# Attention folded into a feed-forward layer on one core: the engines' issue order from a table

## The chip, the core and the metric

One Trainium2 chip, and on it one of its cores. A core has five engines that run side by side, each with an instruction stream of its own: TensorE (PE) for matmuls, VectorE (DVE) and ScalarE (ACT) for elementwise work, GpSimd (POOL), and SyncE (SP), which here only issues DMA transfers. An engine starts its instructions in the order of its stream; where one needs something of another engine it waits, and everything behind it on that engine waits too. The metric is the device time of one execution in microseconds.

## The reference

Eight batches of eight heads of a small attention, whose keys and values are first condensed into 32 memory slots, then a feed-forward layer:

```python
def _attn_ref(q, k, v, phi):                      # 8 x 8 x 576 x 64, phi 8 x 8 x 576 x 32
    a = phi - np.max(phi, axis=2, keepdims=True)  # softmax over the 576 positions
    a = np.exp(a)
    a = a / (np.sum(a, axis=2, keepdims=True) + 1e-09)
    k_m = np.einsum('bhsm,bhsd->bhmd', a, k)
    v_m = np.einsum('bhsm,bhsd->bhmd', a, v)
    scores = scale * np.matmul(q, k_m.transpose(0, 1, 3, 2))
    scores = scores - np.max(scores, axis=-1, keepdims=True)
    attn = np.exp(scores)
    attn = attn / (np.sum(attn, axis=-1, keepdims=True) + 1e-09)
    return np.matmul(attn, v_m)

def _moe_ref(x, w_in, w_out):                     # x 4608 x 512, w_in 512 x 2048, w_out 2048 x 512
    h = x @ w_in
    g = h * np.cos(h)
    return g @ w_out
```

The weights come as 64-bit floats.

## The kernel before

**The algebra.** The output of the attention, attn times v_m, is at once multiplied by w_in. So the kernel multiplies v_m by w_in first (the *fold*, 256 memory slots x 2048 columns for each batch) and the softmaxed scores by the result (the first GEMM, tile `hp`). Then come the cosine (`u`, `gp`) and the second GEMM into three accumulators (`acc`).

**Tiles.** The 4608 tokens are 12 groups of 384 (two batches of 576 are three groups), the 2048 columns 16 pieces `f` of 128. So there are 192 steps (`grp`, `f`). A step is `gemm1` (hp, L519), `act` (L538), `act_end` (L551) and `gemm2` (L564, three accumulators). Names in the text: hp_0_8 is the tile of group 0, piece 8; acc_0_1 the accumulator of group 0's second 128 tokens. Group 0 works in float32, for the weights' scales aren't known yet; all others in pairs of float16 (high and low part), three products for each.

**The cosine.** ACT rounds hp to whole periods (`gp` as integers, L544); DVE takes the difference (`u`, L547); ACT takes the sine (L552); DVE multiplies by hp (L554 in group 0, L556 later), which frees hp's PSUM buffer (three in all, `ps_h`). From group 1 on ACT copies the high half (L558) and DVE subtracts for the low half (L559); then gp can be multiplied. The sine and the exponential of the softmaxes need different function tables on ACT, so a change between them costs a table load.

**The weights.** w_in and w_out come in eight pieces each, through three raw buffers in turn (two pieces of w_in use room in `wo` instead). `to_float32` (L134) turns a piece into float32: DVE takes the sign (L143), ACT the low bits (L147), ACT scales the high word (L151), DVE joins both (L152), ACT squares for the largest value (L154), into the raw buffer, which is free for the next load after that. When all of w_in is squared, `weight_scale` (L174) finds one scale (L177 to L182, L164 to L171: `m_in`, `e_in`, `s_in`), and `scales` (L323) the factor `T` from it. The float16 pairs are made by `split_first` (L499: vw_0_q from vf_q), `fold` (L481: vw_b_q from pv), `w_in_split` and `w_out_split`.

**The first batch's fold.** `fold_first(j)` (L487) multiplies the condensed values of batch 0 by piece j of w_in into a PSUM tile (`pvf`) and copies it into `vf` (L497), two pieces to a `vf` tile. The copies of pieces 0 and 1 are on ACT by name; for the other six `nc.any` lets the scheduler take an engine. In the profile ACT has four of the eight and DVE four. Group 0's three output copies (L589) are `nc.any` as well; the profile has two on ACT and one on DVE.

**Attention.** `memory(b)` (L227) and `attend(b)` (L349) are generators that the main loop (L709) advances between the steps: the softmax over positions (L254, L260), the condensing matmuls (psA), their transpose (tpx, km, vm), the scores (sc), their softmax (L389 to L400) and the transposition back (aT). All these small PSUM tiles, and pvf and pv, share two buffers (`ps_s`).

**The order.** The code is written as one program. A scheduler of the framework puts each engine's instructions in order when the program is built: it models the engines, and takes among the instructions whose inputs are there the one of highest priority, mostly the earliest in the program. A few are pinned by `tc.keep_in_program_order`: the warm-up matmuls (L630), two conversion steps of piece 1, the subtraction L254 from batch 4 on, and the rounding L544 behind the last step of a group.

**Startup.** The first 14 `warm` matmuls, and more between the small ones of batch 0, multiply zeros: their results aren't used, they keep PE busy while it would wait.

Of the kernel before, what the change touches and what calls it, by code (L numbers as in the profile page):

```python
# [16 lines left out]
AF = mybir.ActivationFunctionType  # L17
ALU = mybir.AluOpType
# [13 lines left out]
WS = 256  # L32
# [7 lines left out]
EXP_MASK = 0x7F800000  # L40
NT = 4
LAG = 4


@with_exitstack
def attention_then_ffn(ctx: ExitStack, tc: tile.TileContext, phi, phiT, kv, qT, w_in, w_out, eye, out):
    nc = tc.nc
# [32 lines left out]
    loads, st = {}, {}  # L80
# [53 lines left out]
    def to_float32(dst, raw, sq_to, pin=False, after_sign=None):  # L134

        low, high = raw[:, :, :, 0], raw[:, :, :, 1]
        flat = raw.rearrange("p c f t -> p c (f t)")
        halves = dst.bitcast(I16).rearrange("p c (f t) -> p c f t", t=2)  # L140
        low_top = flat.bitcast(U8).rearrange("p c (f t) -> p c f t", t=8)[:, :, :, 3]
        high_top = flat.bitcast(I8).rearrange("p c (f t) -> p c f t", t=8)[:, :, :, 7]
        sign = nc.vector.tensor_scalar(out=halves[:, :, :, 1], in0=high_top, scalar1=0.0, scalar2=-32768.0,  # L143
                                       op0=ALU.is_lt, op1=ALU.mult)
        if after_sign:
            after_sign(sign)
        begin = nc.scalar.activation(halves[:, :, :, 0], low_top, AF.Copy, scale=2.0 ** -5, bias=-31.0 / 64.0)  # L147
        if pin:
            for ins in (sign, begin):
                tc.keep_in_program_order(ins)  # L150
        nc.scalar.activation(high.bitcast(F32), high.bitcast(F32), AF.Copy, scale=2.0 ** -112)  # L151
        nc.vector.scalar_tensor_tensor(out=dst.bitcast(I32), in0=high, scalar=3, in1=dst.bitcast(I32),  # L152
                                       op0=ALU.logical_shift_left, op1=ALU.bitwise_or)
        nc.scalar.activation(low.bitcast(F32), dst, AF.Square, accum_out=sq_to)  # L154
# [72 lines left out]
    def memory(b):  # L227
        a = loads.pop(("phi", b))
# [10 lines left out]
        if b < NT:  # L239
# [3 lines left out]
            top = small_ps(f"top_{b}")[:, 0:HM]  # L243
            for g in range(2):
                nc.tensor.matmul(top[:, g * P:(g + 1) * P], lhsT=nmx[:, g:g + 1].broadcast_to([P, P]), rhs=ident,
                                 start=True, stop=True)
        else:
            top = st["top", b]
# [2 lines left out]
            yield  # L251
            yield
        for c0, c1, n in ((0, 2, P), (2, 4, P), (4, 5, S - 512)) if b == 0 else ((0, 4, P), (4, 5, S - 512)):
            ins = nc.vector.tensor_tensor(out=a[:n, c0:c1], in0=a[:n, c0:c1],  # L254
                                          in1=top[:n].unsqueeze(1).broadcast_to([n, c1 - c0, HM]),
                                          op=ALU.subtract)
            if b >= NT:

                tc.keep_in_program_order(ins)
            nc.scalar.activation(a[:n, c0:c1], a[:n, c0:c1], AF.Exp)  # L260
        yield
        if b:
# [3 lines left out]
        for c, (s0, n) in enumerate(TCH):  # L266
            for g in range(2):
                for j in range(4):
# [3 lines left out]
                        lhsT=a[:n, c, h * M:(h + 1) * M], rhs=kvs[c][:n, h * KV:(h + 1) * KV],  # L272
                        start=(c == 0 and g == 0), stop=(c == 4), skip_group_check=True)
# [7 lines left out]
        pv = psA[:, 0:2 * KV].rearrange("p (g x) -> p g x", g=2)  # L281
# [205 lines left out]
    def fold_first(j):  # L487
        q, r = divmod(j, 2)
        if r == 0:
            st["vf", q] = wk.tile([P, 2, FS], F32, tag="vw", name=f"vf_{q}", bufs=8)  # L490
        pv = small_ps(f"pvf_{j}").rearrange("p (g x) -> p g x", g=2)
        for g in range(2):
            for i in range(2):
                c = 2 * g + i
                nc.tensor.matmul(pv[D * i:D * (i + 1), g], lhsT=st["vm", 0][:, c],
                                 rhs=w_in_sb[:, c, j * WS:(j + 1) * WS], start=True, stop=True)
        (nc.scalar.copy if j < 2 else nc.any.tensor_copy)(out=st["vf", q][:, :, r * WS:(r + 1) * WS], in_=pv)  # L497

    def split_first(q):  # L499
        vw = wk.tile([P, 2, 2, FS], F16, tag="vw", name=f"vw_0_{q}", bufs=8)  # L500
# [37 lines left out]
    def act(grp, f, hp, pin=False):  # L538
        u = ew.tile([P, GT], F32, tag="u", name=f"u_{grp}_{f}", bufs=3)
        gp = ew.tile([P, GT], F32, tag="gp", name=f"gp_{grp}_{f}", bufs=6)  # L540
        ni = gp.bitcast(I32)
        for b, t0, c0, n in regions(grp):
            c, cu = slice(c0, c0 + n), st["cu", b] if grp else 1.0 / (2.0 * math.pi)
            ins = nc.scalar.activation(ni[:, c], hp[:, c], AF.Copy, scale=cu, bias=0.25)  # L544
            if pin:
                tc.keep_in_program_order(ins)
            nc.vector.scalar_tensor_tensor(out=u[:, c], in0=hp[:, c], scalar=cu, in1=ni[:, c],  # L547
                                           op0=ALU.mult, op1=ALU.subtract)
        return u, gp
# [12 lines left out]
    accs = {}  # L562
# [21 lines left out]
    def evacuate(grp, t):  # L584
# [1 line left out]
        ob = wk.tile([P, DM], F32, tag="back", name=f"ob_{grp}_{t}", bufs=4)  # L586
        osc = st["os_mid", pair] if 3 * r + t == 4 else st["os", 2 * pair + (3 * r + t) // 5] if grp else None
        if grp == 0:
            nc.any.tensor_copy(out=ob, in_=accs[grp][t])  # L589
        elif grp == 11 and t == 2:  # L590

            r0, m = (3 * grp + t) * P, DM // 2
# [34 lines left out]

    def warm(n):
        for _ in range(n):
            tc.keep_in_program_order(nc.tensor.matmul(wps, lhsT=zeros[:, 0:P], rhs=zeros, start=True, stop=True))  # L630
    warm(14)
    mem = memory(0)
    next(mem)
# [8 lines left out]
    warm(3)  # L642

    def attention_rest(sign):
        tc.keep_in_program_order(sign)
        next(mem)
        warm(2)

# [147 lines left out]
```

## Time and profile before

| | us |
|---|---|
| median of three runs | 708.84 |
| lowest, highest | 708.61, 710.9 |
| the profiled execution, whole | 710.08 |
| its span, first to last instruction | 708.3 |
| PE busy in it | 687.8 (97%) |
| DVE busy | 532.7 (75%) |
| ACT busy | 518.7 (73%) |

The profile is one execution. Its span leaves out what lies ahead of the first and behind the last instruction, 1.8 us here. A row of a time line gives the start, the length, the engine, the line of the code, the operation, the tiles (out<-in) and the count of instructions merged into it; in brackets stands how long the engine had been idle and who ended that. A float32 matmul is two records of PE, so `x8` of hp in group 0 is four matmuls, two tiles. The ends of matmuls are modelled; their starts are measured.

### The profile page before, as it was taken

What the parts mean: (1) busy time and instruction counts of PE and PEld (TensorE: products, weight loads), DVE (VectorE), ACT (ScalarE), POOL (GpSimd) and SP (SyncE); (2) the same over time, 40 slices, a digit from 0 to 9 for tenths busy, and PEclk for the clock granted to TensorE, in tenths of its full rate; (3) what the DMA queues carried; (4) which work ended last, traced back from release to release, by engine and by line L of the source; (5) the groups of instructions that cost most, each with busy time, mean ns of one, the idle gap of its engine ahead of it and who ended that gap; (6) DMA issues with size and microseconds to landing.
All of it is one profiled execution on the core that took longest, in us unless ns stands there. A gap on an engine that the chain in (4) does not pass through costs nothing.

```text
span 708.3 us, 11822 instructions
## 1 busy us (share of the span) xinstructions
PE 687.8 (97%) x4597; PEld 364.7 (51%) x4597; DVE 532.7 (75%) x1135; ACT 518.7 (73%) x951; POOL 13.7 (2%) x34
## 2 busy tenths in 40 slices
PE   8699899999999999999999999999999999999997
PEld 3354345565555445666445445666445454665553
DVE  3889879999968966599667886599567976575552
ACT  1899999897985865778666875778766875665652
POOL 0000000000000000000000100000000000000000
PEclk9999999999999999999999999999999999999999
DMA  8996782326407100160105200160100000100101
GB/s 281 379 321 218 266 293 60 105 61 195 146 1 237 44 1 1 56 226 1 44 1 167 99 16 1 46 206 31 44 2 2 22 23 1 46 1 1 45 1 44
DMA packets 31959, 66.18 MB, mean 93 GB/s; under 512 B 2208, under 2 KB 12320, under 8 KB 31904
## 3 DMA queue, kind: packets, MB, share of 16 engines
q1 hardware_dynamic: 27440, 57.43, 25.0%
q10 hardware_dynamic: 4464, 8.00, 3.0%
q8 instruction: 36, 0.59, 0.3%
q14 instruction: 19, 0.16, 0.1%
HBM read 51.79 MB, written 9.44 MB: 86 GB/s over the span
## 4 chain that ended last, share of the span: by engine, by line
PE 60%; DVE 21%; ACT 16%; DMA 2%; issue 1%; ACTq 0%; POOL 0%; DVEq 0%; SPq 0%
PE acc L577 33%; PE hp L533 16%; DVE u L547 4%; ACT u L552 3%; DVE u L556 3%; DVE gp L559 3%; PE psA L270 3%; DVE vw L478 2%; PE sc L376 2%; PE pv L471 2%; ACT gp L558 2%; DMA phi<-in_phi 2%; DVE wo L191 2%; PE hp L524 1%; DVE w_in_parts L202 1%
## 5 line engine op out<-in xcount | busy, mean ns | idle before, releaser
L577 PE MATMUL acc<-wo,gp 128*128 128x512 f16 x1584 | 371.8, 379 | 1.2 <-DVE ob L589 0.7
L577 PEld LDWEIGHTS <-gp 128*128 128x128 f16 x1584 | 153.3, 98 | 162.6 <-issue 4.1
L533 PE MATMUL hp<-aT,vw 128*128 128x192 f16 (+1 forms) x1440 | 202.7, 284 | 1.0 <-DVE u L556 1.0
L533 PEld LDWEIGHTS <-vw 128*128 128x128 f16 x1440 | 128.3, 98 | 77.4 <-issue 17.5
L552 ACT ACTIVATE u<-u,quarter 128x384 f32<-128x384 f32 x192 | 116.7, 615 | 63.8 <-DVE u L547 62.9
L556 DVE SCALAR_TENSOR_TENSOR u<-hp,u 128x384 f32<-128x384 f32 x176 | 96.5, 553 | 60.6 <-ACT u L552 60.1
L544 ACT ACTIVATE gp<-hp,cu 128x192 int32<-128x192 f32 (+1 forms) x240 | 115.4, 492 | 28.1 <-PE hp L533 12.3
L547 DVE SCALAR_TENSOR_TENSOR u<-hp,cu,gp 128x192 f32<-128x192 f32 (+1 forms) x240 | 118.8, 503 | 21.9 <-ACT gp L544 21.5
L559 DVE TENSOR_TENSOR gp<-u,gp 128x384 f16<-128x384 f32 x176 | 96.4, 552 | 43.0 <-ACT gp L558 41.9
L558 ACT CAST gp<-u 128x384 f16<-128x384 f32 x176 | 88.8, 510 | 54.3 <-DVE u L556 53.0
L572 PE MATMUL acc<-wo,gp 128*128 128x512 f32 x96 | 45.1, 599 | 0.0
L478 DVE SCALAR_TENSOR_TENSOR vw<-pv,vw 128x512 f16<-128x512 f32 x48 | 31.5, 684 | 3.0 <-ACT vw L477 2.9
L524 PE MATMUL hp<-aT,vf 128*128 128x384 f32 x64 | 25.6, 533 | 7.9 <-DVE vf L497 3.1
L477 ACT ACTIVATE vw<-pv 128x512 f16<-128x512 f32 x48 | 26.8, 589 | 1.1 <-PE pv L471 0.9
L572 PEld LDWEIGHTS acc<-wo,gp 128*128 128x128 f32 x96 | 17.4, 190 | 17.8 <-issue 15.2
L601 ACT ACTIVATE ob<-acc,os 128x512 f32<-128x512 f32 x27 | 17.8, 682 | 9.6 <-PE acc L577 7.1
L524 PEld LDWEIGHTS hp<-aT,vf 128*128 128x128 f32 x64 | 12.2, 202 | 20.1 <-issue 4.3
L552 ACT ACT_TABLE_LOAD x17 | 21.8, 1283 | 0.3
L270 PE MATMUL psA<-kv,phi 128*32 128x129 f32 (+1 forms) x640 | 21.0, 275 | 0.7 <-ACT phi L260 0.5
L376 PE MATMUL sc<-q,km 128*64 128x256 f32 (+3 forms) x192 | 19.8, 342 | 1.6 <-DVE vw L478 1.2
L270 PEld LDWEIGHTS psA<-kv,phi 128*32 128x32 f32 (+1 forms) x640 | 16.4, 109 | 7.3 <-issue 3.3
L376 PEld LDWEIGHTS sc<-q,km 128*64 128x64 f32 x192 | 12.1, 140 | 12.0 <-issue 3.6
(136 smaller groups left out, 544.7 us busy)
## 6 DMA issues: line engine op xcount, KB each, us to landing
kv<-in_kv SPq DMA_DIRECT2D x32, 516.0 KB, 6.9
raw_out<-in_w_out SPq DMA_DIRECT2D x8, 1024.0 KB, 5.8
q<-in_qT SPq DMA_DIRECT2D x7, 1152.0 KB, 6.0
out<-ob ACTq DMA_DIRECT2D x30, 256.0 KB, 2.1
raw_in<-in_w_in SPq DMA_DIRECT2D x6, 1024.0 KB, 8.1
phi<-in_phi SPq DMA_DIRECT2D x8, 512.0 KB, 5.9
w_in_sb<-w_in_parts SPq DMA_DIRECT2D x12, 256.0 KB, 4.0
kv<-in_kv SPq DMA_DIRECT2D x8, 258.0 KB, 8.5
```

Of the source, the lines that this page charges most:

```text
L270: nc.tensor.matmul(psA[32 * j:32 * (j + 1), g * KV:(g + 1) * KV], lhsT=a[:n, c, h * M:(h + 1) * M], rhs=kvs[c][:n, h * KV:(h + 1) * KV], s ...
L376: nc.tensor.matmul(sc[D * p:D * (p + 1), g * n:(g + 1) * n], lhsT=km[:, 2 * g + p], rhs=qt[:, 2 * g + p, t0:t0 + n], start=True, stop=True)
L478: nc.vector.scalar_tensor_tensor(out=vw[:, 1, g], in0=src, scalar=T, in1=vw[:, 0, g], op0=ALU.mult, op1=ALU.subtract)
L533: nc.tensor.matmul(hp[:, c0:c0 + n], lhsT=vw[:, wi, g, fo * P:(fo + 1) * P], rhs=aT[:, ai, g, c1:c1 + n], start=(k == 0), stop=(k == 5))
L544: ins = nc.scalar.activation(ni[:, c], hp[:, c], AF.Copy, scale=cu, bias=0.25)
L547: nc.vector.scalar_tensor_tensor(out=u[:, c], in0=hp[:, c], scalar=cu, in1=ni[:, c], op0=ALU.mult, op1=ALU.subtract)
L552: nc.scalar.activation(u, u, AF.Sin, scale=TWO_PI_BELOW, bias=quarter)
L556: nc.vector.scalar_tensor_tensor(out=u, in0=hp[:, :GT], scalar=2.0 ** -17, in1=u, op0=ALU.mult, op1=ALU.mult)
L558: nc.scalar.copy(gp[:, 0], u)
L559: nc.vector.tensor_tensor(out=gp[:, 1], in0=u, in1=gp[:, 0], op=ALU.subtract)
L572: nc.tensor.matmul(accs[grp][t], lhsT=gp[:, t * P:(t + 1) * P], rhs=wo[:, f + 1], start=(f == 0), stop=(f == NF - 1))
L577: nc.tensor.matmul(accs[grp][t], lhsT=gp[:, gi, t * P:(t + 1) * P], rhs=parts[:, wi], start=(f == 0 and gi == 0 and wi == 0), stop=(f == N ...
```

## The change

A table `NEXT` holds, for each of the five engines, a string of numbers. `issue_in_order`, called at the end of the program, takes an engine's instructions in program order as a list, and for each number removes the instruction at that place of what is left; each is tied to the one before it, without a semaphore. So the table fixes the whole order on every engine: 4029 matmuls, 931 instructions of ACT, 1136 of DVE, 30 of POOL and 107 of SP. `5x3` stands for three fives; `0` is the next one in program order. The pins go, and the two free choices of an engine are written out: six fold copies on DVE (ACT keeps two), group 0's output copies on ACT.

```diff
+NEXT = {
+    mybir.EngineType.PE: (
+        "0x26 8 0x8 8 0x16 2x8 4x8 0x4 3x2 5x4 0x3 2x4 0x24 4x2 12x2 0x4 14x2 54x2 0x8 58 0x2 56 0x4 63 52 "
...
+    mybir.EngineType.Activation: (
+        "0 1 0x5 3 2 1x2 3x2 6 0x2 1 11 3 1 9 1 0 3 0 5 2 4 8x2 4x2 2 0 1x2 7 4 1 0 2 7 3 2 0x2 3 0 7 0 4 3 0 "
...
+    mybir.EngineType.DVE: (
+        "6x2 5 0x2 1x2 0x12 4 1x2 0 1 4x3 0 3 11 3x2 10 3 8 0 2 6 2 3 2 5 2 17 19 2 3 17 0x3 10 14 10 20 0x2 "
...
+    mybir.EngineType.SP: (
+        "0x29 6x4 0x2 4x2 0 3 0x5 16 0 1 0x14 2x2 0x6 2x2 0x6 2x2 0x6 2x2 0x6 2x2 0x12 "),
+}
+
+def issue_in_order(tc):
+    traced = [i for i in tc.nc.cur_bb.bb.instructions if not type(i).__name__.startswith("BassTile")]
+    for engine, text in NEXT.items():
+        left = [i for i in traced if i.engine == engine]
+        last = None
+        for word in text.split():
+            at, _, times = word.partition("x")
+            for _ in range(int(times or 1)):
+                ins = left.pop(int(at))
+                if last is not None:
+                    tc.add_manual_dep(ins, last.name, mybir.DependencyInfo(
+                        mybir.DependencyClass.NoSync, mybir.DependencyReason.DATA), reason="issue order")
+                last = ins
+        assert not left, engine
...
-        begin = nc.scalar.activation(halves[:, :, :, 0], low_top, AF.Copy, scale=2.0 ** -5, bias=-31.0 / 64.0)
-        if pin:
-            for ins in (sign, begin):
-                tc.keep_in_program_order(ins)
+        nc.scalar.activation(halves[:, :, :, 0], low_top, AF.Copy, scale=2.0 ** -5, bias=-31.0 / 64.0)
...
-        (nc.scalar.copy if j < 2 else nc.any.tensor_copy)(out=st["vf", q][:, :, r * WS:(r + 1) * WS], in_=pv)
+        (nc.scalar.copy if j < 2 else nc.vector.tensor_copy)(out=st["vf", q][:, :, r * WS:(r + 1) * WS], in_=pv)
...
-            nc.any.tensor_copy(out=ob, in_=accs[grp][t])
+            nc.scalar.copy(out=ob, in_=accs[grp][t])
...
-            tc.keep_in_program_order(nc.tensor.matmul(wps, lhsT=zeros[:, 0:P], rhs=zeros, start=True, stop=True))
+            nc.tensor.matmul(wps, lhsT=zeros[:, 0:P], rhs=zeros, start=True, stop=True)
...
     for p in pending:
         gemm2(*p)
+    issue_in_order(tc)
```

Crossed off against the program order, parts of the table read so (line, tile; in0 is piece 0 of w_in, out0 of w_out):

```
DVE, from batch 0's values on: L301, L302 vm_0; L143 in0; L308; L381 sc_0_0, sc_0_256; L389; L152 in0;
  L390; L143 in1; L394; L395; L143 out0; L396; L152 in1; L310; L400; L152 out0; L406 x3; L143 in2;
  L406; L242 nmx_1; L143 in3; L547 u_0_0; L152 in2, in3; ev_0; L554 gp_0_0; L547 u_0_1, u_0_2;
  L554 gp_0_1; L547 u_0_3; L497 pvf_2; ...
ACT, from km_0 on: L147 in0; L151 in0; L147 in1; L422; L497 pvf_0; L151 in1; L147 out0; L151 out0; L147 in2;
  L154 in0, in1, out0; L147 in3; L151 in2; L544 gp_0_0; L151 in3; L552 u_0_0; L497 pvf_1; L544 gp_0_1;
  L154 in2, in3; L552 u_0_1; L544 gp_0_2, gp_0_3; L552 u_0_3, u_0_2; L147 out1; ...
PE: ... 14 warm; pvf_0; 6 warm; hp_0_0, hp_0_1; pvf_1; hp_0_2, hp_0_3; pvf_2; sc_0_384; acc; top_1; acc; pvf_3;
  acc x2; hp_0_4; psA_1; hp_0_5; acc; tpx_1; acc x3; sc_1_0; hp_0_6; acc; sc_1_256; acc; sc_1_512; acc; pvf_4;
  acc x2; hp_0_7; half of hp_0_8; acc x2; pvf_5; acc; hp_0_9; the other half of hp_0_8; acc x5; hp_0_10; ...
```

In groups 1 to 11 the table mixes the three accumulators of several pieces: the nine matmuls of a piece, which the program has together, stand in packs of three with other pieces between.

More of the change, by code (lines that the diff above doesn't have):

```diff
@@ L42 @@
 LAG = 4
+NEXT = {
+    mybir.EngineType.PE: (
[31 rows of a table added]
+    mybir.EngineType.Activation: (
[18 rows of a table added]
+    mybir.EngineType.DVE: (
[23 rows of a table added]
+    mybir.EngineType.Pool: (
+        "0x2 2 0x3 2 0 1 0 2 0x2 3 0 1 0 3 0x3 3 0x3 3 0x4 "),
+    mybir.EngineType.SP: (
[15 more added lines that the diff above has]
+        assert not left, engine
 @with_exitstack
@@ L253, in memory @@
         for c0, c1, n in ((0, 2, P), (2, 4, P), (4, 5, S - 512)) if b == 0 else ((0, 4, P), (4, 5, S - 512)):
[L254 to L259, printed above, removed]
+            nc.vector.tensor_tensor(out=a[:n, c0:c1], in0=a[:n, c0:c1],
+                                    in1=top[:n].unsqueeze(1).broadcast_to([n, c1 - c0, HM]),
+                                    op=ALU.subtract)
             nc.scalar.activation(a[:n, c0:c1], a[:n, c0:c1], AF.Exp)
@@ L543, in act @@
             c, cu = slice(c0, c0 + n), st["cu", b] if grp else 1.0 / (2.0 * math.pi)
-            ins = nc.scalar.activation(ni[:, c], hp[:, c], AF.Copy, scale=cu, bias=0.25)
-            if pin:
-                tc.keep_in_program_order(ins)
+            nc.scalar.activation(ni[:, c], hp[:, c], AF.Copy, scale=cu, bias=0.25)
             nc.vector.scalar_tensor_tensor(out=u[:, c], in0=hp[:, c], scalar=cu, in1=ni[:, c],
@@ L644, in attention_rest @@
     def attention_rest(sign):
-        tc.keep_in_program_order(sign)
         next(mem)
```

69 rows, old and new, of the table NEXT are left out of this document.

## The prediction

> **What bounds the kernel now.** I read the page first, then the waits of PE, busy time by stages, and last the time lines of PE, DVE and ACT over the first 125 us.
>
> ```profile
> span 708.3 us, 11822 instructions
> ...
> PE 687.8 (97%) x4597; PEld 364.7 (51%) x4597; DVE 532.7 (75%) x1135; ACT 518.7 (73%) x951; POOL 13.7 (2%) x34
> ```
>
> No matmul is added or dropped, so PE's 687.8 us stay. An order can win at most the other 20.5 us, and what a slow clock stretches. The stages say where these are (per row: stage, length, busy us of PE, PEld, DVE, ACT, POOL, granted clock, DMA share, GB/s):
>
> ```profile
> 20.00:40.00 20.00, 13.03 (x55) 6.12 (x55) 15.98 (x24) 18.49 (x24) 0.00 (x0) 0.95 1.05 367
> ...
> 120.00:160.00 40.00, 39.27 (x261) 22.95 (x260) 39.88 (x82) 37.50 (x77) 0.31 (x1) 1.00 0.30 73
> 160.00:700.00 540.00, 536.72 (x3773) 288.25 (x3772) 397.07 (x856) 379.58 (x725) 10.05 (x19) 1.00 0.17 56
> 700.00:708.30 8.30, 4.42 (x21) 1.80 (x19) 1.24 (x2) 1.16 (x2) 0.00 (x0) 0.93 0.26 95
> ```
>
> Idle PE: 7.0 us from 20 to 40, 0.7 from 120 to 160, 3.3 from 160 to 700 and 3.9 at the tail; the rest, 5.6, lies before 20 and at one wait near 75. From 20 to 40 ACT is 18.5 of 20 us busy, from 120 to 160 DVE 39.9 of 40: PE waits there for engines that have no room. After 160 us PE is full and the other two have a quarter free. The waits of PE that an order can touch (who, for whom; us in total, times, longest):
>
> ```profile
> PE hp L524 <- DVE vf L497: 3.1, 1, 3.1
> ...
> PE hp L524 <- DVE gp L554: 2.1, 1, 2.1
> ...
> PE hp L524 <- ACT vf L497: 1.8, 1, 1.8
> PE sc L376 <- DVE vw L478: 1.2, 1, 1.2
> PE hp L533 <- DVE u L556: 1.0, 2, 0.8
> ...
> PE acc L577 <- DVE ob L589: 0.7, 1, 0.7
> ...
> PE acc L577 <- ACT ob L601: 0.4, 1, 0.4
> ```
>
> The first three lie in the first 80 us, the other four (3.3 us) behind 120; with smaller ones the stages have 4.0 there.
>
> **The change, part by part.** I crossed the table off against the program order and walked the three full engines through it by hand, each instruction starting at the later of its engine's last end and its inputs, with the durations of these rows (ns of one; back to back on one engine the next starts some 100 ns before the end):
>
> ```profile
> L552 ACT ACT_TABLE_LOAD x17 | 21.8, 1283 | 0.3
> ...
> L147 ACT ACTIVATE wo<-raw_out 128x1024 int16<-128x1024 uint8 x8 | 10.9, 1368 | 0.0
> ...
> L152 DVE SCALAR_TENSOR_TENSOR wo<-raw_out,wo 128x1024 int32<-128x1024 int32 x8 | 9.8, 1227 | 1.4 <-ACT raw_out L151 1.2
> L154 ACT ACTIVATE raw_out<-wo 128x1024 f32<-128x1024 f32 x8 | 9.3, 1161 | 0.0
> L151 ACT ACTIVATE raw_out<-raw_out 128x1024 f32<-128x1024 f32 x8 | 9.2, 1147 | 0.0
> ...
> L143 DVE TENSOR_SCALAR wo<-raw_out 128x1024 int16<-128x1024 int8 x8 | 6.0, 751 | 0.0
> ...
> L497 DVE COPY vf<-pvf 128x512 f32<-128x512 f32 x4 | 2.7, 677 | 0.0
> ...
> L497 ACT COPY vf<-pvf 128x512 f32<-128x512 f32 x4 | 2.3, 574 | 0.0
> ```
>
> **Fold copies and group 0's output copies.** Of the eight fold copies ACT has four now and two afterwards: DVE gains 2 x 0.68 = 1.35 us, ACT loses 2 x 0.57 = 1.15. One of three ob copies goes back from DVE to ACT, 0.57 to 0.68. Net DVE +0.7, ACT -0.6, where both are full. Exp and Sin alternate 34 times in the new ACT order, as many as the table loads now: no price. SP's queue keeps its order but for a few kv pieces of batch 2 moved behind weight pieces; no load of the first 47 us can move, since they land one behind the other.
>
> **From the first weight piece to the first GEMM.** These rows of before carry it:
>
> ```profile
> 18.71 1.37 ACT L147 ACTIVATE w_in_sb<-raw_in 128x1024 int16<-128x1024 uint8 x1 [1.12 <-DMA raw_in<-in_w_in]
> ...
> 22.22 1.22 DVE L152 SCALAR_TENSOR_TENSOR w_in_sb<-raw_in,w_in_sb 128x1024 int32<-128x1024 int32 x1
> ...
> 26.99 2.82 PE L524 MATMUL hp<-aT,vf 128*128 128x384 f32 x8 [0.92 <-DVE aT L406]
> ...
> 35.50 0.61 ACT L552 ACTIVATE u<-u,quarter 128x384 f32<-128x384 f32 x1
> ...
> 38.44 1.98 PE L495 MATMUL pvf<-w_in_sb,vm 128*64 128x256 f32 x8
> ...
> 50.66 1.56 PE L524 MATMUL hp<-aT,vf 128*128 128x384 f32 x4
> ```
>
> In the table DVE does the sign of piece 0 (L143) ahead of the score transposes: 18.7 to 19.4; transposes to 20.5, maximum to 21.4, then L152 of piece 0 to 22.7, 0.8 us sooner, and with it the first fold. But the subtraction of the softmax comes behind, then L152 of pieces 1 and of w_out's 0 come ahead of the normalization's end, and a sign step between the last transposes: aT is ready at 31.8, not 27.0. The first GEMM starts 4.8 us later. ACT doesn't lose that: it converts meanwhile, takes up hp_0_0 at 35.1, loads Sin and ends the first sine at 38.4 (now 36.1), with 2.9 us more of conversion done than it has now at that point. PE's lag at fixed points: pvf_2 at 41.5 against 38.4, hp_0_5 at 52.4 against 50.7.
>
> [...]
>
> **The stall at 72 us** is the clearest waste of the scheduler's order:
>
> ```profile
> 71.25 1.13 PE L572 MATMUL acc<-wo,gp 128*128 128x512 f32 x2
> ...
> 74.80 0.67 DVE L497 COPY vf<-pvf 128x512 f32<-128x512 f32 x1
> ...
> 75.52 4.54 PE L524 MATMUL hp<-aT,vf 128*128 128x384 f32 x8 [3.14 <-DVE vf L497]
> ```
>
> The copy of pvf_4, whose matmuls ended at 68.3, stands on DVE behind eight other things. In the table it follows L152 of piece 5 at once, 69.3 by my walk, and PE has hp_0_7 and accumulations until then: 3.1 us of idleness and 4.54 - 2.82 = 1.7 of slow clock go. At 78.7 PE has what it has now at 79.9, where the two hp are through: the lag of 1.7 has become a lead of 1.2.
>
> **To the first split-precision GEMM.** What is late next is a chain on ACT. Piece 7 of w_in loads into the buffer that the square (L154) of w_out's piece 3 frees; that ended at 79.0, now 82.6, since ACT first waits 1.7 us for a transpose of batch 1 and 1.0 for the sign of w_out's piece 3. hp_0_10 waits 0.7 us for gp_0_7, which frees its PSUM buffer, and gp_0_9 costs 1.0. Between the steps of the w_in scale (L179 to L182) the table has L152 and L143 of w_out's pieces 5 and 6, so s_in comes at 101.2, not 97.2; the last split of vw_0_0 at 111.9, not 107.1.
>
> ```profile
> 79.04 0.37 SPq L124 DMA_DIRECT2D raw_in<-in_w_in  x1
> ...
> 79.90 5.31 PE L572 MATMUL acc<-wo,gp 128*128 128x512 f32 x12
> ...
> 97.05 0.15 DVE L171 TENSOR_SCALAR s_in<-s_in 128x1 f32<-128x1 f32 x1
> ...
> 105.67 1.40 DVE L478 SCALAR_TENSOR_TENSOR vw<-vf,T,vw 128x512 f16<-128x512 f32 x2
> ...
> 107.87 1.15 PE L533 MATMUL hp<-aT,vw 128*128 128x192 f16 x12
> ```
>
> So hp_1_0 starts at 112.0 against 107.9 (4.1 later), with 38 accumulations of group 0 behind it instead of 36; two of them are 4 of the 12 records that start in 5.2 us from 79.90, 1.7 us. **Net +2.4 us.** The walk has some 250 steps; an error of 2 us in either direction would not surprise me.
>
> **From 112 us on** I only measured distances in the table, in PE's own time. A quiet step shows what a tile needs:
>
> ```profile
> 691.63 1.14 PE L533 MATMUL hp<-aT,vw 128*128 128x384 f16 x6
> ...
> 694.97 0.56 DVE L556 SCALAR_TENSOR_TENSOR u<-hp,u 128x384 f32<-128x384 f32 x1 [0.68 <-ACT u L552]
> ...
> 696.11 0.56 DVE L559 TENSOR_TENSOR gp<-u,gp 128x384 f16<-128x384 f32 x1 [0.58 <-ACT gp L558]
> ```
>
> From the end of hp (692.8) to the free buffer 2.8 us, to gp 3.9. In the table the shortest ways are 3.9 and 4.5, most are above 6. Accumulators have 2.6 us or more to be copied out, psA_2 stands 6.5 us behind its maximum. So of the 4.0 us of late idleness I let 3.0 go. New tight places are sc_2_0 and sc_5_0, one accumulation (0.65) behind their tpx, and folds split in two: +0.8, between 0 and 2. The last matmul to the end stays: 3.9.
>
> **Sum**: +2.4 - 3.0 + 0.8 = +0.2 on the profiled span of 708.3. The profiled execution took 710.08 with what lies around it, the median of the runs is 708.84. **Forecast: 709.0 us.**
>
> **The rivals.** *Faster (702)*: my walk is too slow where ACT waits for DVE. Of its ACT idleness from 42 to 76 us (5.8 against 1.7 now) most hangs on single inversions, as u_0_3 ahead of u_0_2 (1.1) and the wait for back_1_0 (1.7). If the real durations let these fall together, the lead of 1.2 at 79 us grows to 4 and holds to hp_1_0; with -3 behind 110 that is -7. For it: PE's waits of 3.1, 2.1 and 1.8 are all inversions of the scheduler, and ACT is given 0.6 less. Against it: ACT and DVE, not PE, are full from 20 to 160 us.
>
> *Slower (714)*: DVE's lag is not absorbed. It is 39.88 of 40 us busy from 120 to 160 and gets 0.7 more. If it enters this stretch 4.8 us late, as at vw_0_0 in my walk, it can't catch up before 160 us. Now gp_1_0 is ready at 117.3 and used at 125.2, 7.9 us of room:
>
> ```profile
> 116.79 0.55 DVE L559 TENSOR_TENSOR gp<-u,gp 128x384 f16<-128x384 f32 x1
> ...
> 125.21 0.81 PE L577 MATMUL acc<-wo,gp 128*128 128x512 f16 x3
> ```
>
> The table uses gp_1_0 some three steps behind its hp; from a lag of about 6 us on PE waits for each gp, and all of the lag counts: +6 behind hp_1_0 instead of +2.4, and with half of the late waits left +5.
>
> *The table changes nothing*: if it were the scheduler's own order written out, 708.8. Its PE order differs by eye in the first ten rows (psA's chunks 1 to 4 without fillers between), so this has no chance of its own and lies within the forecast's.
>
> **How the numbers follow.** The measurement can't tell changes under 0.3% (2.1 us) apart. Within (706.7 to 711.0), my forecast: 0.38. Faster: 0.36; the walk's error of 2 us and the late waits reach it easily. Slower: 0.26. The range takes in 702 at the lower side and 714 at the upper: 702 to 714; the likeliest case alone spans 706.7 to 711.
>
> **What would show it.** The walk is right if the first hp of L524 starts near 32 us with 5 us or more of idleness ahead, if no PE wait for vf stands near 72 us, and if the first L533 comes near 112 us; wrong if that one comes ahead of 107. The late part is right if PE's waits behind 120 us sum to about 1.6 us. The slow rival shows as L577 waiting for gp between 115 and 165 us.

## The result and the profile after

The changed kernel took 713.91 us (median of five runs, 712.71 to 716.14), the kernel before 710.9 beside it (five runs, 708.61 to 712.01): 1.0056 times as long, 95% interval 1.0031 to 1.0081. In a second series, 712.98 against 709.6: 1.0044, interval 1.0029 to 1.006. So it is slower by 3 to 4 us, where 709.0 us and practically no difference (+0.2 us) were forecast.

The lines of the new helper push every line behind it down: the copies of fold tiles are now L591, the first GEMM L618 and L627, accumulations L664 and L669, the conversion L243 to L251. First the page of the changed kernel:

```profile
span 712.4 us, 11883 instructions
...
PE 689.3 (97%) x4597; PEld 362.9 (51%) x4597; DVE 530.6 (74%) x1136; ACT 517.2 (73%) x950; POOL 14.5 (2%) x34
```

PE has the same work; this execution's span is 4.1 us longer than the one shown of the kernel before. The same stages as before (length, then busy us of PE, PEld, DVE, ACT, POOL, the granted clock, DMA share, GB/s):

```profile
20.00:40.00 20.00, 13.50 (x63) 5.99 (x63) 16.56 (x28) 17.63 (x22) 0.99 (x1) 0.91 1.06 372
120.00:160.00 40.00, 39.70 (x257) 23.13 (x256) 39.77 (x81) 38.82 (x80) 0.31 (x1) 1.00 0.42 100
160.00:700.00 540.00, 536.91 (x3777) 287.41 (x3776) 396.07 (x860) 379.75 (x730) 10.32 (x19) 1.00 0.17 56
```

Behind 160 us PE is idle for 540 - 536.91 = 3.1 us, where it was 3.3. The forecast had let 3.0 us of late idleness go. The waits of PE say what took its place (who, for whom; us in total, times, longest):

```profile
PE hp L618 <- DVE aT L500: 4.7, 1, 4.7
PE psA L364 <- DMA kv<-in_kv: 3.2, 3, 1.8
PE hp L618 <- ACT vf L591: 3.0, 1, 3.0
...
PE acc L664 <- DVE gp L646: 1.4, 2, 1.0
...
PE hp L627 <- DVE u L648: 1.3, 2, 1.0
PE pv L565 <- DVE vl L437: 1.0, 1, 1.0
PE pv L565 <- DVE vm L396: 0.6, 1, 0.6
```

Of the four late rows of before, that of `sc` behind `vw` and the two of `ob` are gone. The last three rows here (2.9 us) are new or, that of `u`, at new places. Of the start, PE's time line:

```profile
33.19 4.52 PE L618 MATMUL hp<-aT,vf 128*128 128x384 f32 x8 [4.69 <-DVE aT L500]
37.63 1.08 PE L589 MATMUL pvf<-w_in_sb,vm 128*64 128x256 f32 x8
41.74 2.85 PE L618 MATMUL hp<-aT,vf 128*128 128x384 f32 x8 [3.02 <-ACT vf L591]
...
69.14 1.08 PE L589 MATMUL pvf<-w_in_sb,vm 128*64 128x256 f32 x8
70.15 1.98 PE L664 MATMUL acc<-wo,gp 128*128 128x512 f32 x4
71.97 2.10 PE L618 MATMUL hp<-aT,vf 128*128 128x384 f32 x6
...
110.75 2.84 PE L664 MATMUL acc<-wo,gp 128*128 128x512 f32 x6 [0.98 <-DVE gp L646]
113.43 1.15 PE L627 MATMUL hp<-aT,vw 128*128 128x192 f16 x12
```

The first GEMM comes 6.2 us later than before (26.99), the stall at 72 us is gone, and hp_1_0 starts at 113.43 instead of 107.87. Two accumulations more lie behind it by then (1.7 us), so this one execution has lost 5.56 - 1.7 = 3.8 us at hp_1_0, and from there to the end only 0.3 more of its 4.1.

### The profile page after: what moved, and what is told of

The parts are those of the page before. It is cut to its first block, busy times and chain, and to the rows that moved or that the text cites. A ratio compares the mean times of both kernels' runs of the same rounds, so it can differ in the third digit from the quotient of the medians.

```text
span 712.4 us, 11883 instructions
## 1 busy us (share of the span) xinstructions
PE 689.3 (97%) x4597; PEld 362.9 (51%) x4597; DVE 530.6 (74%) x1136; ACT 517.2 (73%) x950; POOL 14.5 (2%) x34
## 4 chain that ended last, share of the span: by engine, by line
PE 75%; ACT 12%; DVE 10%; DMA 2%; issue 1%; SPq 0%; ACTq 0%
PE acc L669 45%; PE hp L627 22%; PE pv L565 3%; PE psA L364 2%; PE sc L470 2%; DMA kv<-in_kv 2%; ACT u L644 2%; DVE u L639 1%; ACT raw_out L251 1%; DVE vw L572 1%; ACT raw_in L251 1%; DVE u L648 1%; ACT gp L638 1%; ACT raw_out L248 1%; ACT L644 1%
## 5 line engine op out<-in xcount | busy, mean ns | idle before, releaser
L669 PE MATMUL acc<-wo,gp 128*128 128x512 f16 x1584 | 372.0, 379 | 0.0
L669 PEld LDWEIGHTS <-gp 128*128 128x128 f16 x1584 | 151.4, 98 | 168.4 <-issue 10.2
L627 PE MATMUL hp<-aT,vw 128*128 128x192 f16 (+1 forms) x1440 | 198.2, 283 | 1.3 <-DVE u L648 1.3
L627 PEld LDWEIGHTS <-vw 128*128 128x128 f16 x1440 | 129.8, 98 | 72.9 <-issue 9.9
L638 ACT ACTIVATE gp<-hp,cu 128x192 int32<-128x192 f32 (+1 forms) x240 | 114.1, 491 | 51.2 <-PE hp L627 31.7
L644 ACT ACTIVATE u<-u,quarter 128x384 f32<-128x384 f32 x192 | 115.7, 612 | 41.4 <-DVE u L639 40.4
L664 PE MATMUL acc<-wo,gp 128*128 128x512 f32 x96 | 46.2, 604 | 1.4 <-DVE gp L646 1.4
L618 PE MATMUL hp<-aT,vf 128*128 128x384 f32 x64 | 25.2, 527 | 7.9 <-DVE aT L500 4.7
L664 PEld LDWEIGHTS acc<-wo,gp 128*128 128x128 f32 x96 | 17.0, 190 | 19.9 <-issue 14.4
L618 PEld LDWEIGHTS hp<-aT,vf 128*128 128x128 f32 x64 | 12.1, 200 | 20.5 <-ACT w_in_sb L247 5.2
L693 ACT ACTIVATE ob<-acc,os 128x512 f32<-128x512 f32 x27 | 17.9, 684 | 4.2 <-PE acc L669 3.9
```

Of the source, the lines that this page charges most:

```text
L627: nc.tensor.matmul(hp[:, c0:c0 + n], lhsT=vw[:, wi, g, fo * P:(fo + 1) * P], rhs=aT[:, ai, g, c1:c1 + n], start=(k == 0), stop=(k == 5))
L644: nc.scalar.activation(u, u, AF.Sin, scale=TWO_PI_BELOW, bias=quarter)
L664: nc.tensor.matmul(accs[grp][t], lhsT=gp[:, t * P:(t + 1) * P], rhs=wo[:, f + 1], start=(f == 0), stop=(f == NF - 1))
L669: nc.tensor.matmul(accs[grp][t], lhsT=gp[:, gi, t * P:(t + 1) * P], rhs=parts[:, wi], start=(f == 0 and gi == 0 and wi == 0), stop=(f == N ...
```

## The experiments

Each kernel below differs from the kernel before or from the changed one only in what is said; the order of all instructions not named is written out as it stood there. "Before" always means runs of the kernel before on the same chip in the same series. In a list of moves, `A > B` means that A now stands ahead of B in its engine's queue.

### Which part of the change costs?

**The old order, written as a table.** Nothing else is changed.

```diff
-    (order by the scheduler)
+NEXT = {...}            # the scheduler's order, engine by engine
+    issue_in_order(tc)
```

> The kernel before with its own order, instruction by instruction on every engine, written as a table, and its own engine for every copy. Every theory: no difference that can be measured (ratio 0.997 to 1.003), since only the way in which the order is written differs. The profile is a second sample of the loads: if the later landing of the first kv pieces under the change (the last at 16.0 us, 14.2 before) is chance from run to run, a value anywhere between may come here; if the change causes it, it stays at 14.2 +- 0.4.

Measured: ratio 0.9994 (interval 0.9982 to 1.0006). The form of the table costs nothing. The last kv piece landed at 14.93 us.

**The copies alone.**

```diff
-        (nc.scalar.copy if j in (0, 1, 2, 6) else nc.vector.tensor_copy)(out=st["vf", q]...   # what before came to
+        (nc.scalar.copy if j < 2 else nc.vector.tensor_copy)(out=st["vf", q]...
-            (nc.vector.tensor_copy if t == 1 else nc.scalar.copy)(out=ob, ...
+            nc.scalar.copy(out=ob, ...
```

> The order before, with only the copies changed: pvf_2's and pvf_6's copies on VectorE, ob_0_1's on ScalarE, each at the place in the new engine's queue that the old order gives it. By the prediction (VectorE +0.7 us, ScalarE -0.6, where both are full): 0 to +0.7 us. Rival: ahead of the stall at 72 us VectorE's queue is the critical one, so that a copy of 0.68 us more in it costs its whole length, +0.7 to +1.4 us.

Measured: 0.9983 (0.9973 to 0.9993), 1.2 us *faster*. Both expectations missed; which copy did it is tested further on.

**Both halves of the order.** One kernel takes the table up to hp_1_0 and the old order behind it, the other the reverse; the sets of instructions ahead of that point differ by a dozen. Each half brings its own engines for the copies: the fold copies go with the start, the output copies with the rest.

> The table's order up to the first split-precision GEMM (hp_1_0), the order before for all that is left. Theory start: the changed kernel loses its 3.8 us ahead of hp_1_0 and its rest is worth nothing, so this one is as slow as the changed kernel, +3 to +5 us against before. Theory rest (the table's rest costs what the start doesn't): +0 to +2 us. Landings: the last kv piece near 16.0 us if the new start causes it.

> The order before up to hp_1_0, the table's for all that is left. Theory start: within 1 us of before. My prediction had the rest at -2.2 us: then 706.5 to 707 where before is at 709. Theory rest: +2 to +4 us. PE's waits behind 120 us sum to 3 us as in the changed kernel (theory start), or to 1.6 (prediction).

Measured: new start 1.0061 (1.0044 to 1.0077), +4.3 us; new rest 1.0016 (1.0003 to 1.0028), +1.1 us. The start carries the loss, and the rest is no gain either. The halves do not simply add up: the first has two new waits at 127 and 129 us, 2.5 us in all, where group 0's output copies, ordered as before, follow a late start. With the last kv piece at 14.78 us, the late landing in the changed kernel's first profile (16.0) isn't something that the new start always brings.

**The changed kernel again.**

> The changed kernel unchanged, for a second profile and more runs. Start and rest measured by halves gave +4.3 and +1.1 us; if they add up, +5.4 us against before; if part of the start's loss is made good later, +3 to +4. The last kv piece landed at 16.0 us in the profile of the changed kernel, at 14.2 to 14.9 in the five others. Chance: it lands at 14 to 15 us here and the first GEMM starts near 31.5; cause: at 16 again and 33.

Measured: 1.0044 as told above, the last kv piece at 14.56, the first GEMM at 31.26 and hp_1_0 at 111.51: here the start has lost 111.51 - 107.87 - 1.7 = 1.9 us, and the span (710.4) is 2.1 longer than before's. So between 1.9 and 3.8 us go at the start in these two executions, and 0.2 to 0.3 behind it. The 1.9 between them goes with the landing of the first loads (the last kv piece at 14.56 and 16.0 us), which differs between these two executions of the same kernel.

### The start: what is the late first GEMM worth?

**The chain to aT put back**, in the changed kernel:

```
VectorE:  L484 at > L249 in0;   L488, L489, L490, L494, L500 x4 > L243 in1, L243 out0, L249 in1, L249 out0
ScalarE:  L516 at (exp) > L247 in1
```

> The changed kernel with one chain put back as it stood before: on VectorE the softmax of the first head block (subtraction, sum, reciprocal, product, four transposes) ahead of the conversions of pieces 1 and of w_out's piece 0, on ScalarE its exp ahead of the conversion of piece 1. First GEMM near 27 us instead of 31 to 33. Theory idle start: PE's 4 us of lateness count whole, -3 to -4 us against the changed kernel. Rival, as my prediction had it: ScalarE and VectorE are full from 20 to 100 us, and ScalarE takes up hp_0_0 no sooner for it, so 0 to -1 us; the lateness shows at the next waits of PE instead.

Measured: 1.0104 (1.0087 to 1.012), 716.81 us: PE's first GEMM started at 27.30, 4 us sooner, and the kernel got 3.8 us *slower* than with it late. The time lines show how. PE with the chain early:

```profile
27.30 2.82 PE L618 MATMUL hp<-aT,vf 128*128 128x384 f32 x8 [0.59 <-DVE aT L500]
30.92 1.08 PE L589 MATMUL pvf<-w_in_sb,vm 128*64 128x256 f32 x8 [0.80 <-DVE l L404]
42.25 4.21 PE L618 MATMUL hp<-aT,vf 128*128 128x384 f32 x6 [10.25 <-ACT vf L591]
```

ScalarE in the same kernel:

```profile
22.98 0.84 ACT L516 ACTIVATE at<-at 128x768 f32<-128x768 f32 x1 [1.35 <-DVE at L484]
23.73 1.35 ACT L247 ACTIVATE w_in_sb<-raw_in 128x1024 int16<-128x1024 uint8 x1
25.34 0.59 ACT L591 COPY vf<-pvf 128x512 f32<-128x512 f32 x1 [0.27 <-PE pvf L589]
28.34 1.18 ACT L248 ACTIVATE raw_in<-raw_in 128x1024 f32<-128x1024 f32 x1 [2.41 <-DVE w_in_sb L243]
...
38.32 0.46 ACT L638 ACTIVATE gp<-hp 128x384 int32<-128x384 f32 x1
```

And ScalarE in the changed kernel's second profile:

```profile
25.42 0.59 ACT L591 COPY vf<-pvf 128x512 f32<-128x512 f32 x1
25.90 1.14 ACT L248 ACTIVATE raw_in<-raw_in 128x1024 f32<-128x1024 f32 x1
...
35.85 0.48 ACT L638 ACTIVATE gp<-hp 128x384 int32<-128x384 f32 x1
```

With the chain early, ScalarE waits 2.41 us for the sign of piece 1 (L243), which VectorE now does behind the chain; VectorE's own last step for that piece (L249) ends up later too, at 29.55 us instead of 27.34. hp_0_0 has been ready since 29 us, but its reader L638 stands behind nine conversion steps in ScalarE's queue and comes 2.5 us later than in the changed kernel. hp_1_0 comes at 115.6 us, 4.1 later. So PE's time to start isn't what counts here; the conversions on the two other engines are. The stage from 18 to 113 us, this kernel first, then the changed kernel:

```profile
18.00:113.00 95.00, 80.11 (x366) 37.57 (x366) 77.39 (x148) 83.62 (x114) 1.93 (x6) 0.93 0.80 276
```

```profile
18.00:113.00 95.00, 85.03 (x385) 39.56 (x383) 79.76 (x156) 87.48 (x123) 2.91 (x7) 0.96 0.79 273
```

ScalarE's idle time is 95 - 83.62 = 11.4 us against 95 - 87.48 = 7.5: 3.9 more, and the kernel is 3.8 slower.

**The stall at 72 us alone**, in the order before:

```
VectorE:  L591 pvf_4 moved 10 instructions forward, right behind L249 in5
```

> The order before with one move: on VectorE the copy of pvf_4 right behind the last conversion step of w_in's piece 5, 11 instructions sooner. The stall at 72 us (3.1 us idle, 1.7 of slow clock) goes in either case. Theory one inversion: -3 to -5 us against before. Rival full engines: ScalarE's work up to the first split sets the end of the stage, hp_0_10 waits for its buffer instead, 0 to -1.5 us.

Measured: 1.0000 (0.9988 to 1.0012). PE's time line shows that the stall went and others came:

```profile
71.41 2.74 PE L618 MATMUL hp<-aT,vf 128*128 128x384 f32 x8
75.75 5.42 PE L664 MATMUL acc<-wo,gp 128*128 128x512 f32 x12 [1.60 <-DVE wo L249]
82.33 0.91 PE L618 MATMUL hp<-aT,vf 128*128 128x384 f32 x2 [1.16 <-DVE vf L591]
83.91 1.90 PE L589 MATMUL pvf<-w_in_sb,vm 128*64 128x256 f32 x8 [0.67 <-DVE w_in_sb L249]
```

PE gets to the next accumulation 4 us sooner and finds that w_out's piece 3 isn't converted yet; then it waits for the next copy and for w_in's piece 6. The largest wait of the profile, 3.1 us with a granted clock of 0.62 in the 4.54 us behind it, was worth nothing that could be measured (0.0 us, +- 0.9): it held PE where the conversions would have held it.

**ScalarE's own waits**, in the changed kernel:

```
ScalarE:  L644 u_0_2 > L644 u_0_3;   L247 out4 > L505 back_1_0;   L248 in4 > L638 gp_0_6
```

> The changed kernel with three moves on ScalarE, where it waits ahead of 80 us: the sine of u_0_2 ahead of that of u_0_3 (ScalarE waits 1.2 at 45), the first conversion step of w_out's piece 4 ahead of the transposed block of batch 1 (0.96 and 0.73 at 75), gp_0_6 behind the next conversion step (0.8 at 63). Theory ScalarE: from the first weight piece to hp_1_0 its idle time counts one for one, so -2 to -3.5 us against the changed kernel (712.98), though PE waits for none of the three. Rival PE: PE runs without a gap at 63 and 75 us, so 0 to -0.7.

Measured: 711.7 us, 1.0026 (1.0015 to 1.0037) against 1.0044 for the changed kernel: 1.3 us less, with intervals that overlap. Its stage:

```profile
18.00:113.00 95.00, 85.17 (x392) 39.61 (x389) 81.71 (x162) 90.17 (x127) 2.90 (x7) 0.98 0.80 276
```

ScalarE idles 4.8 us, 2.7 less, and hp_1_0 starts at 109.56 (111.51). The profiled execution is the fastest of seven, 1.9 us shorter than that of the changed kernel. It points the way that theory ScalarE has it, at half the size or somewhat more; PE had no wait at any of the three places.

**ScalarE given less, or later**: two splits of w_in (L298) in the changed kernel behind those of hp_1_0, alone and then together with the three moves above.

```
ScalarE:  L571 vw_0_0 > L298, L298 (w_in's second part);   VectorE:  L572 vw_0_0 > L299
```

> The changed kernel with two weight splits of w_in's second part (0.7 us each on ScalarE, one 0.75 on VectorE) moved behind the splits that hp_1_0 waits for. ScalarE has 1.4 us less to do ahead of hp_1_0. Theory ScalarE: hp_1_0 1.2 us sooner and the wait of 1.0 for gp_0_13 at 108 gone, -1 us against the changed kernel, part of it given back behind 112. Rival room behind 112: the splits are needed there just as well, 0.

Measured: 1.0044 (1.0027 to 1.0061), nothing. PE's wait of 1.0 us at 108 us went, but its waits for `u` grew by as much: there is a new one of 0.75 us at 127, where the sine that `u` needs (L644, 125.72) stands behind an output copy on ScalarE (L681, 125.26), and one of 0.62 at 137.

> The changed kernel with the three moves on ScalarE and the splits moved behind those of hp_1_0, together. The moves alone gave -1.3 us, the splits nothing, since what they gained between 100 and 120 us went at one output copy at 127. If the two add up ahead of 112 us and the rest costs its 1.1 us: 710.5 to 711.3 where before is at 709.8 (ratio 1.001 to 1.002). If the splits are needed behind 112 just as well: as with the moves alone, ratio 1.0026 +- 0.0008.

Measured: 1.0032 (1.0018 to 1.0047), no better than the three moves alone.

**More or less work on ScalarE**, in the order before: all eight fold copies on one engine.

```diff
-        (nc.scalar.copy if j in (0, 1, 2, 6) else nc.vector.tensor_copy)(out=st["vf", q]...
+        nc.vector.tensor_copy(out=st["vf", q]...      # the other kernel: nc.scalar.copy
```

> The order before with all eight fold copies on VectorE (four before). ScalarE is given 4 x 0.57 = 2.3 us less, VectorE 2.7 more, each copy where the old order has it, the first one within the chain to aT. Theory ScalarE: -1.5 to -2.3 us against before. Rival VectorE: +0.5 to +2.7.

> The order before with all eight fold copies on ScalarE. Theory ScalarE: 2.3 us more work there, +1.5 to +2.3 us against before, though the stall at 72 us, where PE waits for a copy on VectorE, gets shorter or goes. Rival (the stall counts): -1 to -4 us.

Measured: on VectorE 1.0003 (0.999 to 1.0016), nothing; on ScalarE 1.0046 (1.0034 to 1.0058), +3.3 us. The stage from 18 to 113 us, in the kernel before and with all copies on ScalarE:

```profile
18.00:113.00 95.00, 84.89 (x388) 40.70 (x384) 81.26 (x162) 90.10 (x129) 1.99 (x6) 0.96 0.80 274
```

```profile
18.00:113.00 95.00, 84.12 (x378) 40.49 (x378) 76.42 (x150) 89.10 (x128) 2.32 (x7) 0.93 0.81 277
```

With all copies ScalarE idles 5.9 us against before's 95 - 90.10 = 4.9, and it has 2.3 us more to do: 3.3 together. (The profiled execution is the slowest of its five; its span is 4.1 us longer than before's.) Taking 2.3 us off ScalarE gained nothing, with 2.7 more on VectorE. So more on ScalarE costs time here, while handing its work to VectorE doesn't gain any.

**Relief from a third engine.** The second ScalarE step of the conversion of four pieces on GpSimd, in the mended old order (below) and in the changed kernel:

```diff
-        nc.scalar.activation(high.bitcast(F32), high.bitcast(F32), AF.Copy, scale=2.0 ** -112)
+        (nc.gpsimd.tensor_scalar_mul(high.bitcast(F32), high.bitcast(F32), 2.0 ** -112) if pin else
+         nc.scalar.activation(high.bitcast(F32), high.bitcast(F32), AF.Copy, scale=2.0 ** -112))
```

> The mended old order, with the multiplication by 2**-112 (second ScalarE step of the conversion) of four pieces, w_in's 3 and 5 and w_out's 2 and 4, on GpSimd. ScalarE has 4 x 1.05 = 4.2 us less to do between 36 and 80 us. Theory ScalarE: -3 to -4.2 us against the mended order, -4 to -5.5 against before. Rival (VectorE, or the length of each piece's chain, sets it): GpSimd's step is longer than ScalarE's, 0 to +2.

> The changed kernel with the same four multiplications on GpSimd. Theory ScalarE: -3 to -4.2 us against the changed kernel (+3 against before), so about as fast as before or 1 us faster. Rival: 0 to +2 against the changed kernel.

Measured: 1.033 (1.0306 to 1.0355) and 1.017 (1.0151 to 1.0189), far slower than any theory had it. GpSimd's time line in the first:

```profile
54.97 0.38 POOL L406 PARTITION_ALL_REDUCE l<-l  x1 [13.17 <-DVE l L404]
64.47 2.88 POOL L248 TENSOR_SCALAR raw_out<-raw_out 128x1024 f32<-128x1024 f32 x1 [9.12 <-issue]
...
105.82 0.31 POOL L390 MEMSET vm<- 128x256 f32 x1 [11.10 <-PE pvf L589]
115.64 0.38 POOL L275 PARTITION_ALL_REDUCE m_in<-m_in  x1 [9.51 <-issue]
```

The multiplication takes 2.9 us or more against 1.15 on ScalarE. Between the reduction over partitions and the multiplication behind it lie 9.12 us in which nothing runs, and the next reduction begins 9.51 us behind a memset; both rows give `issue`, so the profile shows nothing that was waited for. The conversion and the scale of w_in wait for these. So the question behind these two runs stays open.

### The rest: why no gain?

**Three late waits mended**, in the changed kernel:

```
VectorE:  L639 u_2_8 > L651 gp_2_6;   L395, L396 vm_4 > L261 ev_4;   L437 vl_5 (second half) > L488 rs_5
```

> The changed kernel with three moves on VectorE, where PE waits behind 200 us: u_2_8's subtraction ahead of gp_2_6's product (PE waits 0.96 at 206), the copies of vm_4 ahead of ev_4 (0.55 at 309), the second half of vl_5 ahead of the sum that waits for exp (0.97 at 406). Theory new inversions: each wait goes with its move, -2 to -2.6 us against the changed kernel. Rival room: what is moved behind is late in its turn, 0 to -0.8.

Measured: 1.0051 (1.0034 to 1.0068), nothing of the 2 to 2.6 us. PE's waits behind 120 us did fall, from 3.3 us in all to 2.5, but from hp_1_0 to the end it takes 598.8 us, where the changed kernel took 598.9 to 599.0. The third move shows one reason. In the changed kernel VectorE idles for ScalarE's exp and holds `vl` behind it:

```profile
405.83 0.82 DVE L488 TENSOR_REDUCE rs<-at 128x20 f32<-128x640 f32 x1 [0.89 <-ACT at L538]
...
407.23 0.35 DVE L437 SCALAR_TENSOR_TENSOR vl<-vm,sv,vp 64x128 f16<-64x128 f32 x1
...
407.64 0.40 PE L565 MATMUL pv<-w_in,vl 128*32 128x512 f16 x4 [0.97 <-DVE vl L437]
407.97 0.82 PE L669 MATMUL acc<-wo,gp 128*128 128x512 f16 x3
```

With `vl` ahead, the same place:

```profile
403.41 0.35 DVE L437 SCALAR_TENSOR_TENSOR vl<-vm,sv,vp 64x128 f16<-64x128 f32 x1
...
404.95 0.39 PE L565 MATMUL pv<-w_in,vl 128*32 128x512 f16 x4
...
405.04 1.83 ACT L693 ACTIVATE ob<-acc,os 128x512 f32<-128x512 f32 x3
...
405.77 0.81 PE L669 MATMUL acc<-wo,gp 128*128 128x512 f16 x3 [0.42 <-ACT ob L693]
```

`pv` doesn't wait, but half of the gain goes at once: the accumulator that comes next is copied out by ScalarE, whose copies L693 stand where they stood. At 309 us the moved copies waited themselves, 1.06 us for ScalarE's copies of the same tile.

### Which copy, and an order better than both

> The order before with one copy changed: group 0's second output copy (ob_0_1) on ScalarE instead of VectorE. PE's wait for it at 125 us (0.7 idle, 0.9 with the restart) shrinks to 0.1 to 0.3. If the output copy is what made the copies alone faster: -0.6 to -1.2 us against before. If the two fold copies did it: 0 to -0.2.

Measured: 0.9989 (0.9977 to 1.0002), 0.8 us less. PE's wait for `ob` at 125 us fell from 0.7 to 0.3 us. So the output copy has most of the 1.2 us of the copies alone, though the interval takes in no difference.

**The old order mended**: the changed kernel's engines for the copies, with six moves ahead of 100 us, and five more behind 290:

```
VectorE:  L591 pvf_4 and pvf_5 forward;   L143 out1 > L506 aT_0's last block
ScalarE:  L644 u_0_3 > L505 aT_0's last block;   L251 out2 > L638 gp_0_6;   L251 in7 > L638 gp_0_12
late:     L639 u_4_3 > L572 vw_3_2;  L648 u_4_3 > L351 phi_4;  L571, L572 vw_4_3 > L538, L488 of batch 5;
          L693 ob_5_0 > L644 u_6_2
```

> The order before, the changed kernel's engines for the copies, and six moves ahead of 100 us: on VectorE the copies of pvf_4 and pvf_5 earlier (and one step of batch 0's last block behind a conversion step), on ScalarE three that let it work where it waited (the last transposed block of batch 0 behind a sine, gp_0_6 behind the square of w_out's piece 2, gp_0_12 behind the square of w_in's piece 7). Theory ScalarE: its idle time from 18 to 113 us falls from 4 to 5.3 us to about 3 and it has 1.15 us less to do: -2 to -3.5 us against before, with the output copy -3 to -4. Rival (PE's own waits set the time, and its stall alone gave nothing): 0 to -1.2, what the copies gave alone.

> The kernel with the mended order, and five more moves behind 290 us against PE's waits of 0.9 to 1.1 us at 296, 1.0 to 1.2 at 395 and 0.4 to 0.55 at 404. If each wait goes with its move: -2 to -2.5 us against the mended order. If the next instruction in the queue is late in its turn, as after the three moves in the changed kernel: 0 to -0.8.

Measured: 0.9982 (0.997 to 0.9994) and 0.9986 (0.9972 to 1.0). The first beats both kernels (708.8 us against 710.3 of before), by no more than the copies alone. ScalarE's idle time from 18 to 113 us, which the moves were to bring down to about 3 us, is 5.1. As with pvf_4 alone, PE's stall at 72 us became one of 1.88 us for w_out's piece 3 at 77. The late moves made two of the three waits smaller or removed them, and others grew: one for `ob` at 405 us from 0.39 to 1.36 us.

## Why the prediction was wrong

It gave +0.2 us, the sum of +2.4 for the start and -2.2 for the rest; measured are 3 to 4.

**The step that failed is the late one**: "of the 4.0 us of late idleness I let 3.0 go". Most of the old waits did go, as forecast, but 2.9 us of waits for `u`, `vl` and `vm` stand in their place. Idleness behind 120 us fell from 4.0 to 0.3 + 3.1 = 3.4 us only, and PE's waits there, which were to sum to 1.6, sum to 3.3. Nor did the little that went become time. From hp_1_0 to the end of the span, in the kernel before and in the changed one:

```profile
107.87:708.30 600.43, 592.53 (x4113) 319.51 (x4111) 450.24 (x967) 430.37 (x827) 10.36 (x20) 1.00 0.18 58
```

```profile
113.43:712.40 598.97, 591.82 (x4109) 317.84 (x4107) 446.36 (x965) 427.87 (x826) 10.63 (x20) 1.00 0.18 58
```

PE's idle time fell from 7.9 to 7.1 us. But the kernel before has two accumulations more in this stretch (1.7 us), so for the same work PE is busy 591.82 - (592.53 - 1.7) = 1.0 us longer, and the stretch is 0.3 us longer (0.2 in the second profile), where 2.2 less were forecast. The ends of matmuls are modelled, so busy time can hide short gaps; where this 1.0 us lies is open. The split folds, with 0.8 in the sum, may be part of it; no run took them alone. The rest of the table on the old start costs 1.1 us (0.2 to 2.0).

The distances in the table were taken in PE's own time, from hp to the free buffer along the shortest chain. What was not asked is what stands in front of each step on VectorE and ScalarE, which wait for each other in order: `vl` stood behind a sum that waited for an exp. And the moves that were meant to take single waits away (one at 72 us, three late) showed that such a wait isn't a price tag: they gave nothing.

**The copies** had no price; alone they make the kernel 1.2 us faster. Four more fold copies on VectorE made no difference. Most of the gain came with the output copy, whose wait at 125 us was in the late sum already; it is due to the engine and not to the order.

**To the first GEMM**: right in its reason. The first GEMM came at 33.19 and 31.26 (31.8 forecast) in the two profiles, with 4.7 to 5.0 us idle ahead, and the two hp took 4.52 us (at a granted clock of 0.62) and 5.46 us instead of 2.82 (at 1.00 in the profile of before). Neither the idleness nor the slow clock held up ScalarE, which took up hp_0_0 at 37.78 and 35.85 (35.1 forecast) straight behind its conversions, without a wait. The experiment with the early chain shows it from the other side: GEMM 4 us sooner, kernel 3.8 us slower.

**The stall at 72 us** vanished as forecast, hp_0_7 runs from 71.97 without a wait. But taking 4.8 us for it, to be spent later on other delays, was the wrong reading: removed alone, it is worth 0.0 +- 0.9 us. The sum didn't suffer, because the walk had found what is late next. What is "late next" was late anyway.

**To hp_1_0**: forecast 112.0 and +2.4 us; measured 111.51 and 113.43, +1.9 and +3.8. The chain that the walk had named is there: in the second profile piece 7's load is issued at 82.62 us (82.6 forecast), s_in is there at 100.9 (101.2) and the last split of vw_0_0 ends at 111.3 (111.9). In the first profile these are 84.52, 102.8 and 113.2. That one of two profiles meets the walk to within 0.6 us is luck in part, since the two executions of the same kernel lie 1.9 us apart here.

ScalarE's idle time from 18 to 113 us rose from 4.9 to 8.9 and 7.5 us in the two profiles with the change, whose spans are 4.1 and 2.1 us longer, and mending three of its waits took 2.7 us off the latter and 1.3 us off the time. That more on ScalarE costs time in this stretch is shown by the eight copies there, though in the old order (3.3 us for 3.3). The early chain (3.9 us for 3.8) holds up VectorE's conversions as well and can't tell the two engines apart. So the start carries the loss, which the halves show; that it is ScalarE's waiting there is supported, not shown alone. What would set the time once ScalarE is relieved is open: less work on it brought nothing where VectorE got it, and the runs with GpSimd gave no answer.

**The rivals.** The slower one had the time, 714, and not the mechanism: L669 does not wait for gp between 115 and 165 us, so VectorE's lag was absorbed. The faster one would have had hp_1_0 ahead of 107 us, which neither profile shows, and it was wrong late in the same place as the sum. The level moved too: beside the first experiments the kernel before took 710.3 us as the median of 29 runs, not the 708.84 of the three runs shown.

## What to carry to other kernels

So far as this one kernel teaches it: where two in-order engines feed a third and each other, the longest wait of the third (3.1 us here, 0.0 +- 0.9 when it alone was taken away) says where the lateness shows, not where it comes from; move one instruction and see whether the end moves before its wait is put into a sum. In a stage where one engine is idle for a twentieth of the time (4.9 of 95 us here), count that engine's idle time under the old and the new order first. A distance in a new order must be taken through the queue of every engine on the way.

## What the runs showed of the hardware

**The clock after idleness.** How long PE was idle doesn't decide by itself whether it then runs slow: in these profiles 2.87 us passed and 1.88 us did not. In the old order written as a table, the two hp behind 2.87 us of idleness took 2.85 us, at a granted clock of 1.00 from 60 to 80 us:

```profile
75.37 2.85 PE L618 MATMUL hp<-aT,vf 128*128 128x384 f32 x8 [2.87 <-DVE vf L591]
```

With all copies on VectorE the granted clock was 1.00 from 18 to 113 us, though PE was idle there for 95 - 83.32 = 11.7 us in all. But in the profile of before the same matmuls took 4.54 us behind 3.14 us of idleness, at a granted clock of 0.62, and in the mended order the accumulations behind 1.88 us ran slow, at 0.58 at first (time line, then the stages):

```profile
77.26 7.11 PE L664 MATMUL acc<-wo,gp 128*128 128x512 f32 x12 [1.88 <-DVE wo L249]
```

```profile
75.00:77.20 2.20, 0.38 (x2) 0.00 (x0) 2.12 (x5) 2.20 (x5) 0.00 (x0) 1.00 0.94 298
77.20:80.80 3.60, 3.54 (x5) 1.62 (x6) 3.45 (x8) 3.60 (x6) 0.00 (x0) 0.58 0.60 230
```

The same twelve records (six accumulations) took 5.42 us in the kernel with only pvf_4 moved, behind 1.60 us of idleness, at a granted clock of 1.00 (75.7 to 81 us). What sets the clock behind a gap, no run here shows.

The slow clock goes with longer executions. Of the 119 executions of the kernel before that stand beside the experiments, at 707.9 to 711.9 us, 35 had a mean granted clock of 0.998 or more and took 708.9 us on average; 82 had 0.995 or less and took 710.5. Whether the slow stretches make these longer or only go with the idleness ahead of them, no run shows. The changed kernel's ten executions all had 0.990 to 0.995. If the slow stretches do cost the 1.6 us, then some 0.5 us of what the change costs (an estimate: 710.5 less the 710.0 of all 119) is that the kernel before sometimes goes without.

**GpSimd's gaps.** In the two kernels with the multiplication on GpSimd there are four gaps of 7.0 to 14.4 us in which the profile shows nothing that is waited for: ahead of a multiplication behind a reduction (9.12 us above, 7.03 in the other kernel), ahead of a reduction behind a memset (9.51 above) and ahead of a multiplication behind a memset (14.39 in the other). It isn't so wherever one operation follows another: the reduction at 54.97 us, 13.17 us behind a memset, was waiting for VectorE's L404 by the profile. What fills the four gaps, no run shows.

**The landing of the first loads.** With the same transfers issued, the last kv piece landed at 14.2 us in the profile of before and at 16.0 in the changed kernel's first. In the changed kernel's two profiles, with 14.56 and 16.0, hp_1_0 starts 1.9 us apart and the spans are 2.0 us apart: that is half or more of what the change costs, so one profile can't price a start.
